# Chunked attention and feed-forward block: mean by a running sum, variance by squares on ScalarE, key/query turns two head pairs at once, first mem values as fp32

## The chip, the cores and the metric

One core of one Trainium2 chip. The metric is the device time of one execution in microseconds (us), the median of several runs. The span of a profile, from its first to its last instruction, is about 1.7 us shorter than the same run's time (246.6 against 248.29). Compare spans with spans and medians with medians.

A ratio in this document is the mean time of one kernel's fast runs over that of the kernel before in the same rounds, so it is not quite the ratio of the two medians quoted beside it.

## The reference

Attention over chunks of 32 rows. Each chunk sees 8 memory keys, 16 rows to the left, its own 32 and 8 to the right. Then comes a layer norm without bias and a feed-forward of 512 to 2048 to 512, with a residual. Sizes: 4 batches, 8 heads, 768 rows, 64 per head.

```python
k_full = np.concatenate([mem_k, k_ctx], axis=2); v_full = np.concatenate([mem_v, v_ctx], axis=2)
a = softmax(scale * q_c @ k_full^T); out_c = a @ v_full          # per chunk of 32 rows (condensed)
mu = mean(x); var = mean((x - mu)**2)
xn = (x - mu) / np.sqrt(var + 1e-06) * g_ln
out = x + np.maximum(xn @ w_ch1, 0.0) @ w_ch2
```

## The kernel before

The 24 tiles of 128 rows are worked in eight units of three. While a unit's feed-forward runs on TensorE (16 "up" steps, one for each 128 of the 2048 hidden columns, then 12 "down" steps), the attention of the next unit's tiles is woven in at fixed steps. Instructions stand in program order on each engine, so one that waits holds back those behind it. The parts that the change touches:

```python
def kq_block(b, j, g0, g1, kind):            # one pair of heads
    if kind == "att":
        p = slot("att")                      # one PSUM tile of two banks
        pk, pq = as16(p[:, 0, :]), as16(p[:, 1, :])
    else:
        pk, pq = as16(slot("mm")[:, :]), as16(slot("mm")[:, :])
    turn_kq(pk, k16[b % 2], j, 96)           # TensorE: transposes of keys
    turn_kq(pq, q16[b % 2], j, 96)           # ... of queries
    keep_k(...)                              # VectorE: copies to KT
    for par in range(2):
        keep_q(nc.scalar.copy, ...)          # ScalarE: copies to QZ

def values(b, t, xi):
    # ... 16 value products into an att slot, 65 columns a head, the 65th the sum of weights
    nc.vector.reciprocal(out=r, in_=...)
    nc.vector.tensor_tensor(out=x, in0=p, in1=r, op=ALU.mult)
    nc.vector.bn_stats(out=bst[i], in_=x)
    nc.vector.bn_aggr(out=m, in_=bst[i])
    nc.vector.scalar_tensor_tensor(out=xn[i], in0=x, scalar=m[:, 0:1], in1=g_row,
                                   op0=ALU.subtract, op1=ALU.mult)
    # root(), later on GpSimd: rstd = (m[:, 1] + 1e-6) ** -0.5, used in the last down step
```

A "turn" is a transpose on TensorE. PSUM is the memory that TensorE writes its products to. Its "slots" go round: two of two banks (att) for scores, values and turns, four of one bank (mm) for the feed-forward. In the lines below, KT and QZ are the turned keys and queries, AT the exps of the scores, V the values, xs and xn a tile's attention before and after the norm, xT the turned xn, rT the relus, w1c and w2c the feed-forward's weights (w1 and w2), and busy the zeros of the filler products. The prologue loads keys, queries, memory values and V, puts the memory values into V with a DMA from SBUF to SBUF (V<-memv), runs three tiles of attention, and fills TensorE's idle time with products of zeros (`stay_busy`).

The softmax here doesn't subtract the row's maximum and nothing guards it: scores larger than these inputs give would overflow.

Of the kernel before, what the change touches and what calls it, by code (L numbers as in the profile page):

```python
# [15 lines left out]
def kernel(  # L16
# [12 lines left out]
    nc = tc.nc  # L29
# [15 lines left out]
    memk16 = sb.tile([128, 2, 64], FP16, name="memk16")  # L45
    memv16 = sb.tile([72, B, H, HD], FP16, name="memv16")[64:72, :, :, :]
    memKT = sb.tile([128, B * 4, 8], FP16, name="memKT")
    g_row = sb.tile([128, 512], FP32, name="g_row")
# [17 lines left out]
    osb = [sb.tile([128, 512], FP32, name=f"osb{i}") for i in range(3)]  # L66
    bst = [sb.tile([128, 6], FP32, name=f"bst{i}") for i in range(3)]
    mv = [sb.tile([128, 2], FP32, name=f"mv{i}") for i in range(6)]
    veps = [sb.tile([128, 1], FP32, name=f"veps{i}") for i in range(3)]
    rstd = [sb.tile([128, 1], FP32, name=f"rstd{i}") for i in range(9)]  # L70
    rec = [sb.tile([128, 2, 4], FP32, name=f"rec{i}") for i in range(2)]

# [17 lines left out]
    def as16(t):  # L90
        return t.bitcast(FP16)
# [110 lines left out]

    def kq_block(b, j, g0, g1, kind):
        if kind == "att":
            p = slot("att")
            pk, pq = as16(p[:, 0, :]), as16(p[:, 1, :])
        else:
            pk, pq = as16(slot("mm")[:, :]), as16(slot("mm")[:, :])
        turn_kq(pk, k16[b % 2], j, 96)
        turn_kq(pq, q16[b % 2], j, 96)  # L210
        keep_k(pk, b, j, 96, g0 + 1 if g0 else 0, g1)
        for par in range(2):
            keep_q(nc.scalar.copy, pq, b, j, par, 96, g0, g1)

# [19 lines left out]
    def values(b, t, xi):  # L234
        x = xs[xi]
        p = slot("att")
        for h in range(H):
            for gg in range(2):
                c0 = HD * (h % 4)
                nc.tensor.matmul(  # L240
                    out=p[64 * gg : 64 * gg + 64, h // 4, c0 : c0 + HD],
                    lhsT=AT[t % 3][0:KR, gg, h, :],
                    rhs=V[b % 2][0:KR, 2 * t + gg, h, :],
                    start=(h % 4 == 0), stop=(h % 4 == 3), tile_position=(0, 64 * gg),
                )
        r = rec[t % 2]
        nc.vector.reciprocal(out=r, in_=free(p, 64, [[512, 2], [HD, 4]]))  # L247
        nc.vector.tensor_tensor(  # L248
            out=x.rearrange("p (a h d) -> p a h d", a=2, h=4),
            in0=free(p, 0, [[512, 2], [HD, 4], [1, 64]]),  # L250
            in1=free(r, 0, [[4, 2], [1, 4], [0, 64]]),
            op=ALU.mult,
        )
        i, m = t % 3, mv[t]
        nc.vector.bn_stats(out=bst[i], in_=x)  # L255
        nc.vector.bn_aggr(out=m, in_=bst[i])  # L256
        nc.vector.scalar_tensor_tensor(  # L257
            out=xn[i], in0=x, scalar=m[:, 0:1], in1=g_row, op0=ALU.subtract, op1=ALU.mult,
        )

    def root(t, xi):
        i = t % 3
        nc.gpsimd.tensor_scalar(  # L263
            out=veps[i], in0=mv[t][:, 1:2], scalar1=1e-6, scalar2=1.0,
            op0=ALU.add, op1=ALU.mult,
        )
        nc.gpsimd.tensor_tensor(out=rstd[xi], in0=veps[i], in1=mhalf, op=ALU.pow)
# [13 lines left out]

    def stay_busy(n):

        p = slot("mm")
        for _ in range(n):
            nc.tensor.matmul(out=p, lhsT=busy[:, 0:128], rhs=busy, start=True, stop=True)  # L286
# [68 lines left out]
    nc.vector.memset(memv16[:, :, :, 64:65], 1.0)  # L355
    nc.sync.dma_start(out=memk32, in_=dram(mem_k, 0, [[64, 128], [128 * 64, 2], [1, 64]]))
    for h in (0, 4):
        for which in range(2):
            load_kq(0, which, 0, CUT, h, h + 4)
    keep(counts[:, 0:1], counts[:, 0:1], 24, 0.0)  # L360
    keep(counts[:, 1:2], counts[:, 1:2], -88, 0.0)
    make_identity(nc, identity)
    nc.gpsimd.dma_start(
        out=memv16[:, :, :, 0:64], in_=dram(mem_v, 0, [[64, 8], [512, B * H], [1, 64]])
    )
    nc.scalar.copy(out=memk16, in_=memk32)
    stay_busy(10)
    clear_v(0)
    clear_k(0)
    mem_keys()  # L370
    mem_cols(0)
    for par in range(2):
        clear_q(0, par)
    stay_busy(8)
    v_mem(0)
# [14 lines left out]
    load_w1(512, 1024)  # L390
    load_w1(1024, 2048)
    load_kq(0, 0, CUT, 96)
    load_kq(0, 1, CUT, 96)
# [7 lines left out]
    load_w2(3)  # L401

    first_k = [as16(slot("mm")[:, :]) for j in range(4)]
    pair = [slot("att"), slot("att")]
    first_q = [as16(pair[j // 2][:, j % 2, :]) for j in range(4)]
    vec, act = nc.vector.tensor_copy, nc.scalar.copy
    for half in ((0, 1), (2, 3)):
        for j in half:
            turn_kq(first_k[j], k16[0], j, CUT)
        for j in half:  # L410
            turn_kq(first_q[j], q16[0], j, CUT)
        for j in half:
            keep_k(first_k[j], 0, j, CUT, 0, 7, act if j == 2 else vec)
        for j in half:
            for par in range(2):
                keep_q(vec if par and j > 1 else act, first_q[j], 0, j, par, CUT, 0, 6)
        stay_busy(9 if half[0] == 0 else 3)
    nc.vector.memset(mhalf, -0.5)
    scores(0, 0)
    scores(0, 1)  # L420
    stay_busy(3)
    values(0, 0, 0)
    scores(0, 2)
    stay_busy(2)
    values(0, 1, 1)
    stay_busy(3)
    values(0, 2, 2)
    stay_busy(2)
    turn_x(0, 0, 0, "mm")
    stay_busy(6)  # L430
    turn_x(0, 1, 1, "mm")
    stay_busy(6)
    turn_x(0, 2, 2, "mm")
# [5 lines left out]
    for u, tiles in enumerate(units):  # L439
# [7 lines left out]
        def attend(steps):  # L447

            for i, (s0, s1, s2) in enumerate(steps):
                t = following[i]  # L450
                at(s0, scores, t // 6, t % 6)
                at(s1, values, t // 6, t % 6, t % 9)
                at(s2, turn_x, u + 1, i, t % 6)
                at(s2, root, t % 6, t % 9)

        if u == 0:
# [3 lines left out]
            at(11, clear_k, 1)  # L460
            for j in range(4):
                at(11 + 3 * (j // 2), kq_block, 0, j, 6, NG, "att")
# [7 lines left out]
        elif u == 1:  # L470
            for j in range(4):
                at(3 + 5 * (j // 2), kq_block, 1, j, 0, NG, "att")
            for g in range(6, NG):
                at(0, load_v_group, 1, g)
            for which in range(2):
                at(1, load_kq, 2, which)
            attend(((12, 16, 20), (16, 18, 23), (20, 22, 26)))
        elif following:
            steps = [(1 + 7 * i, 5 + 7 * i, 11 + 7 * i) for i in range(3)]
            attend(steps)  # L480
            if u in (2, 4):
                b = u // 2 + 1
                for j, step in enumerate((steps[1][1], steps[2][1], steps[2][1], 23)):
                    at(step, kq_block, b, j, 0, NG, "mm" if j == 1 else "att")
                for h in range(H):
# [48 lines left out]
```

## Time and profile before

| | before |
|---|---|
| median time | 248.62 us (248.06 to 249.05) |
| span of the profile | 246.6 us |
| first value product | 21.29 us |
| first feed-forward product | 31.26 us |
| VectorE, one tile's norm (reciprocal to end of xn) | 2.66 us |
| ScalarE busy | 41% |

The row to start from is TensorE's 93%: nothing off TensorE counts unless TensorE waits for it. The waits are in two places, before 31.26 us and in short stalls after it. The prediction below shows the lines. The share of busy time by engine doesn't tell where they are; the chain in order of time and the list of waits do.

### The profile page before, as it was taken

To read this page: it belongs to the slowest core of one execution; us is meant where nothing else is said; L and a number is where in the kernel's file an instruction comes from. 1 tells how busy PE (TensorE), PEld (TensorE's weight loads), DVE (VectorE), ACT (ScalarE), POOL (GpSimd) and SP (SyncE) were. 2 spreads that over 40 slices of the span, in tenths; PEclk is the share of its full clock that TensorE was granted. 3 is DMA by queue.
4 is the path that set the end of the run, shared out by engine and by line. 5 is a ranking of instruction groups with operands and counts; after the bars stand their busy time and mean duration, and the time that the engine had idled before them with its cause. 6 is when DMAs were issued, how large, how long until landed. Compare 5 with 4: busy or idle time off the path is not lost.

```text
span 246.6 us, 5414 instructions
## 1 busy us (share of the span) xinstructions
PE 228.9 (93%) x2264; PEld 137.9 (56%) x2264; DVE 141.4 (57%) x287; ACT 100.7 (41%) x178; POOL 74.9 (30%) x122
## 2 busy tenths in 40 slices
PE   7765999998989999989999999989999999999992
PEld 2443467655765566655665566655765576547540
DVE  3733868278665757747375637776574457444221
ACT  2353235731585334284554045356453045303300
POOL 7862138627501283303022525220022202220000
PEclk9996799999999999999999999999999999999999
DMA  5999999999995199928930194541100110021012
GB/s 85 138 138 222 209 194 163 194 175 98 179 173 88 45 97 71 48 57 115 214 64 3 48 124 55 33 95 56 43 3 12 73 45 0 4 85 43 0 43 85
DMA packets 44279, 22.29 MB, mean 90 GB/s; under 512 B 32432, under 2 KB 39984, under 8 KB 44208
## 3 DMA queue, kind: packets, MB, share of 16 engines
q0 software_dynamic: 39872, 14.39, 72.1%
q1 hardware_dynamic: 4384, 7.57, 10.7%
q8 instruction: 17, 0.28, 0.5%
q14 instruction: 6, 0.05, 0.1%
HBM read 29.10 MB, written 6.29 MB: 144 GB/s over the span
## 4 chain that ended last, share of the span: by engine, by line
PE 73%; DVE 9%; DMA 7%; ACT 6%; issue 2%; POOL 1%; ACTq 0%; DVEq 0%; POOLq 0%; SPq 0%
PE mm L295 29%; PE mm L312 29%; PE att L173 4%; PE att L240 4%; DMA V<-memv 3%; ACT QZ L198 3%; DMA memv<-in_mem_v_dram 3%; PE att L221 3%; PE mm L286 2%; DVE KT L188 2%; PE att L272 2%; DVE xn L257 2%; DVE bst L255 1%; DVE xs L248 1%; ACT AT L228 1%
## 5 line engine op out<-in xcount | busy, mean ns | idle before, releaser
L295 PE MATMUL mm<-xT,w1c 128*128 128x384 f16 x512 | 90.6, 327 | 3.0 <-ACT xT L277 1.9
L312 PE MATMUL mm<-w2c,rT 128*128 128x512 f16 x384 | 89.4, 380 | 0.0
L295 PEld LDWEIGHTS <-w1c 128*128 128x128 f16 x512 | 56.3, 114 | 27.7 <-issue 4.9
L312 PEld LDWEIGHTS <-rT 128*128 128x128 f16 x384 | 35.6, 98 | 37.8 <-ACT rT L301 1.0
L263 POOL TENSOR_SCALAR veps<-mv 128x1 f32<-128x1 f32 x24 | 16.3, 677 | 121.8 <-DVE mv L256 121.6
L303 DVE TENSOR_SCALAR rT<-mm 128x384 f16<-128x384 f32 x64 | 34.9, 555 | 30.1 <-PE mm L295 30.0
L301 ACT ACTIVATE rT<-mm 128x384 f16<-128x384 f32 x64 | 30.9, 489 | 46.2 <-PE mm L295 38.5
L319 DVE SCALAR_TENSOR_TENSOR osb<-mm,rstd,xs 128x512 f32<-128x512 f32 x24 | 17.9, 748 | 40.0 <-issue 20.7
L228 ACT ACTIVATE AT<-att,band 96x512 f16<-96x512 f32 x48 | 30.1, 678 | 11.0 <-PE att L221 10.9
L198 ACT COPY QZ<-att 64x768 f16<-64x768 f16 (+1 forms) x34 | 22.5, 661 | 28.0 <-DVE KT L188 20.8
L277 ACT COPY xT<-att 128x512 f16<-128x512 f16 x21 | 12.3, 584 | 36.2 <-PE att L272 36.1
L109 POOL DMA_DIRECT2D V<-in_v_dram x24 | 18.3, 769 | 12.3 <-DMA w1c<-in_moe_w_ch_dram 7.9
L286 PE MATMUL mm<-busy 128*128 128x512 f16 x52 | 17.0, 471 | 2.6 <-DVE KT L188 1.4
L257 DVE SCALAR_TENSOR_TENSOR xn<-xs,mv,g_row 128x512 f16<-128x512 f32 x24 | 18.0, 752 | 0.9
L221 PE MATMUL att<-QZ,KT 128*128 128x128 f16 x192 | 15.6, 223 | 2.7 <-ACT QZ L198 1.5
L255 DVE BATCH_NORM_STATS2 bst<-xs 128x6 f32<-128x512 f32 x24 | 16.7, 695 | 0.8
L248 DVE TENSOR_TENSOR xs<-att,rec 128x512 f32<-128x512 f32 x24 | 16.6, 692 | 0.8
L188 DVE COPY KT<-att 128x80 f16<-128x80 f16 (+3 forms) x38 | 16.1, 481 | 1.6 <-PE att L173 1.6
L240 PEld LDWEIGHTS <-AT 96*64 96x64 f16 x384 | 8.7, 116 | 14.6 <-issue 8.0
L221 PEld LDWEIGHTS <-KT 128*128 128x128 f16 x192 | 12.8, 100 | 5.8 <-issue 3.1
L240 PE MATMUL att<-V,AT 96*64 96x65 f16 x384 | 11.5, 204 | 5.0 <-DMA V<-memv 3.6
L247 DVE RECIPROCAL rec<-att 128x8 f32<-128x8 f32 x24 | 4.9, 203 | 17.9 <-PE att L240 17.0
(52 smaller groups left out, 126.9 us busy)
## 6 DMA issues: line engine op xcount, KB each, us to landing
out_dram<-osb SPq DMA_DIRECT2D x24, 256.0 KB, 2.0
V<-in_v_dram POOLq DMA_DIRECT2D x36, 96.0 KB, 7.4
k<-in_k_dram POOLq DMA_DIRECT2D x3, 768.0 KB, 10.5
q<-in_q_dram POOLq DMA_DIRECT2D x3, 768.0 KB, 14.2
w2c<-in_moe_w_ch_dram POOLq DMA_DIRECT2D x4, 512.0 KB, 17.7
w1c<-in_moe_w_ch_dram POOLq DMA_DIRECT2D x2, 512.0 KB, 10.2
w1c<-in_moe_w_ch_dram POOLq DMA_DIRECT2D x1, 1024.0 KB, 16.2
k<-in_k_dram POOLq DMA_DIRECT2D x3, 256.0 KB, 5.7
```

The source lines that it names most:

```text
L188: copy(out=free(KT[b % 2], j * KC + 24 + 32 * ga + 8 * lo, [[KR, gb - ga], [8, m], [1, 8]]), in_=free(pv, lo, [[8, gb - ga], [1, m], [n, 8]]),
L198: copy(out=free(QZ[b % 2][rows, j, g0, par, :], 0, [[128, g1 - g0], [8, 8], [1, 8]]), in_=free(pv[rows, :], 8 * g0, [[8, g1 - g0], [1, 8], ...
L221: nc.tensor.matmul(out=p[:, gg, 128 * j : 128 * j + 128], lhsT=KT[b % 2][:, j, KR * g : KR * g + 128], rhs=QZ[b % 2][:, j, g, :, :], start ...
L228: nc.scalar.activation(out=free(a, 32 * c, [[512, 2], [64, 8], [1, 32]], KR), in_=free(p, 32 * c, [[512, 2], [64, 8], [1, 32]], KR), func= ...
L240: nc.tensor.matmul(out=p[64 * gg : 64 * gg + 64, h // 4, c0 : c0 + HD], lhsT=AT[t % 3][0:KR, gg, h, :], rhs=V[b % 2][0:KR, 2 * t + gg, h, ...
L255: nc.vector.bn_stats(out=bst[i], in_=x)
L257: nc.vector.scalar_tensor_tensor(out=xn[i], in0=x, scalar=m[:, 0:1], in1=g_row, op0=ALU.subtract, op1=ALU.mult,)
L286: nc.tensor.matmul(out=p, lhsT=busy[:, 0:128], rhs=busy, start=True, stop=True)
L295: nc.tensor.matmul(out=p, lhsT=free(w, i, [[4, 128]]), rhs=xT[u % 2][:, dt, 0 : 128 * n], start=(dt == 0), stop=(dt == 3),)
L301: nc.scalar.activation(out=o, in_=p, func=ACTF.Relu)
L303: nc.vector.tensor_scalar(out=o, in0=p, scalar1=0.0, scalar2=None, op0=ALU.max)
L312: nc.tensor.matmul(out=p, lhsT=rT[hc][:, 128 * i : 128 * i + 128], rhs=w2c[hc // 4][:, hc % 4, :], start=(hc == 0), stop=(hc == 15),)
```

## The change

The intent is a shorter start and less work on VectorE in the steady part. (1) mem_v of batch 0 comes as fp32 on the hardware queue and is cast by ScalarE; the other batches follow later on the software queue. (2) The norm's mean is the accumulated sum of the product that makes x, and its variance is a Square on ScalarE with an accumulator; bn_stats and bn_aggr go. (3) A key/query block turns two pairs of heads, keys in one PSUM tile, queries in another, at other steps. (4) The prologue's clears, turns, copies and filler products are put in another order and partly cut.

```diff
+    nc.sync.dma_start(out=memv32, in_=dram(mem_v, 0, [[64, 8], [512, H], [1, 64]]))
...
+    nc.scalar.copy(out=memv16[:, 0, :, 0:64], in_=memv32.rearrange("p (h d) -> p h d", h=H))
     stay_busy(10)
+    for par in range(2):
+        clear_q(0, par)
+    clear_k(0)
     clear_v(0)
-    clear_k(0)
...
-        nc.vector.bn_stats(out=bst[i], in_=x)
-        nc.vector.bn_aggr(out=m, in_=bst[i])
         nc.vector.scalar_tensor_tensor(
+            out=x.rearrange("p (h d) -> p h d", h=H),
+            in0=free(p, 0, [[128, H], [1, 64]]), scalar=1.0,
+            in1=free(r, 0, [[1, H], [0, 64]]),
+            op0=ALU.mult, op1=ALU.mult, accum_out=total[i],
+        )
+        nc.vector.tensor_scalar(
+            out=nmean[i], in0=total[i], scalar1=-1.0 / 512, scalar2=None, op0=ALU.mult,
+        )
...
     def root(t, xi):
+        nc.scalar.activation(
+            out=junk, in_=xs[xi], func=ACTF.Square, bias=nmean[i], accum_out=squares[i],
+        )
...
     def kq_block(b, j, g0, g1, kind):
+        pk, pq = slot("att"), None
         if kind == "att":
+            pq = slot("att")
+            pq = [pq[:, i, :] for i in range(2)]
         else:
+            pq = [slot("mm")[:, :] for i in range(2)]
+        for i in range(2):
+            turn_kq(as16(pk[:, i, :]), k16[b % 2], j + i, 96)
+        for i in range(2):
+            turn_kq(as16(pq[i]), q16[b % 2], j + i, 96)
...
     turn_x(0, 0, 0, "mm")
-    stay_busy(6)
+    stay_busy(4)
     turn_x(0, 1, 1, "mm")
...
-                for j, step in enumerate((steps[1][1], steps[2][1], steps[2][1], 23)):
-                    at(step, kq_block, b, j, 0, NG, "mm" if j == 1 else "att")
+                for j, step in ((0, 19), (2, 22)):
+                    at(step, kq_block, b, j, 0, NG, "mm")
```

More of the change, by code (lines that the diff above doesn't have):

```diff
@@ L46 @@
     memv16 = sb.tile([72, B, H, HD], FP16, name="memv16")[64:72, :, :, :]
+    memv32 = sb.tile([72, 512], FP32, name="memv32")[64:72, :]
     memKT = sb.tile([128, B * 4, 8], FP16, name="memKT")
@@ L66 @@
     osb = [sb.tile([128, 512], FP32, name=f"osb{i}") for i in range(3)]
-    bst = [sb.tile([128, 6], FP32, name=f"bst{i}") for i in range(3)]
-    mv = [sb.tile([128, 2], FP32, name=f"mv{i}") for i in range(6)]
+    total = [sb.tile([128, 1], FP32, name=f"total{i}") for i in range(3)]
+    nmean = [sb.tile([128, 1], FP32, name=f"nmean{i}") for i in range(3)]
+    squares = [sb.tile([128, 1], FP32, name=f"squares{i}") for i in range(3)]
+    junk = sb.tile([128, 512], FP16, name="junk")
     veps = [sb.tile([128, 1], FP32, name=f"veps{i}") for i in range(3)]
     rstd = [sb.tile([128, 1], FP32, name=f"rstd{i}") for i in range(9)]
-    rec = [sb.tile([128, 2, 4], FP32, name=f"rec{i}") for i in range(2)]
+    rec = [sb.tile([128, 8], FP32, name=f"rec{i}") for i in range(2)]
     att = [ps.tile([128, 2, 512], FP32, name=f"att{i}") for i in range(2)]
@@ L203, in kq_block @@
     def kq_block(b, j, g0, g1, kind):
+        pk, pq = slot("att"), None
         if kind == "att":
-            p = slot("att")
-            pk, pq = as16(p[:, 0, :]), as16(p[:, 1, :])
-        else:
-            pk, pq = as16(slot("mm")[:, :]), as16(slot("mm")[:, :])
-        turn_kq(pk, k16[b % 2], j, 96)
-        turn_kq(pq, q16[b % 2], j, 96)
-        keep_k(pk, b, j, 96, g0 + 1 if g0 else 0, g1)
-        for par in range(2):
-            keep_q(nc.scalar.copy, pq, b, j, par, 96, g0, g1)
+            pq = slot("att")
+            pq = [pq[:, i, :] for i in range(2)]
+        else:
+            pq = [slot("mm")[:, :] for i in range(2)]
[3 more added lines that the diff above has]
+            turn_kq(as16(pq[i]), q16[b % 2], j + i, 96)
+        for i in range(2):
+            keep_k(as16(pk[:, i, :]), b, j + i, 96, g0 + 1 if g0 else 0, g1)
+        for i in range(2):
+            for par in range(2):
+                keep_q(nc.scalar.copy, as16(pq[i]), b, j + i, par, 96, g0, g1)
     def scores(b, t):
@@ L238, in values @@
             for gg in range(2):
-                c0 = HD * (h % 4)
+                c0 = 128 * (h % 4)
                 nc.tensor.matmul(
@@ L245, in values @@
                 )
-        r = rec[t % 2]
-        nc.vector.reciprocal(out=r, in_=free(p, 64, [[512, 2], [HD, 4]]))
-        nc.vector.tensor_tensor(
-            out=x.rearrange("p (a h d) -> p a h d", a=2, h=4),
-            in0=free(p, 0, [[512, 2], [HD, 4], [1, 64]]),
-            in1=free(r, 0, [[4, 2], [1, 4], [0, 64]]),
-            op=ALU.mult,
-        )
-        i, m = t % 3, mv[t]
-        nc.vector.bn_stats(out=bst[i], in_=x)
-        nc.vector.bn_aggr(out=m, in_=bst[i])
+        r, i = rec[t % 2], t % 3
+        nc.vector.reciprocal(out=r, in_=free(p, 64, [[128, H]]))
+        nc.vector.scalar_tensor_tensor(
+            out=x.rearrange("p (h d) -> p h d", h=H),
+            in0=free(p, 0, [[128, H], [1, 64]]), scalar=1.0,
+            in1=free(r, 0, [[1, H], [0, 64]]),
+            op0=ALU.mult, op1=ALU.mult, accum_out=total[i],
+        )
+        nc.vector.tensor_scalar(
+            out=nmean[i], in0=total[i], scalar1=-1.0 / 512, scalar2=None, op0=ALU.mult,
+        )
         nc.vector.scalar_tensor_tensor(
-            out=xn[i], in0=x, scalar=m[:, 0:1], in1=g_row, op0=ALU.subtract, op1=ALU.mult,
+            out=xn[i], in0=x, scalar=nmean[i], in1=g_row, op0=ALU.add, op1=ALU.mult,
         )
@@ L262, in root @@
         i = t % 3
+        nc.scalar.activation(
+            out=junk, in_=xs[xi], func=ACTF.Square, bias=nmean[i], accum_out=squares[i],
+        )
         nc.gpsimd.tensor_scalar(
-            out=veps[i], in0=mv[t][:, 1:2], scalar1=1e-6, scalar2=1.0,
-            op0=ALU.add, op1=ALU.mult,
+            out=veps[i], in0=squares[i], scalar1=1.0 / 512, scalar2=1e-6,
+            op0=ALU.mult, op1=ALU.add,
         )
@@ L280, in turn_x, with stay_busy @@
         )
-    def stay_busy(n):
-        p = slot("mm")
+    def stay_busy(n, p=None):
+        p = slot("mm") if p is None else p
         for _ in range(n):
@@ L362 @@
     make_identity(nc, identity)
-    nc.gpsimd.dma_start(
-        out=memv16[:, :, :, 0:64], in_=dram(mem_v, 0, [[64, 8], [512, B * H], [1, 64]])
-    )
     nc.scalar.copy(out=memk16, in_=memk32)
+    nc.scalar.copy(out=memv16[:, 0, :, 0:64], in_=memv32.rearrange("p (h d) -> p h d", h=H))
     stay_busy(10)
+    for par in range(2):
+        clear_q(0, par)
+    clear_k(0)
     clear_v(0)
-    clear_k(0)
     mem_keys()
     mem_cols(0)
-    for par in range(2):
-        clear_q(0, par)
-    stay_busy(8)
+    stay_busy(5)
     v_mem(0)
@@ L391 @@
     load_w1(1024, 2048)
+    nc.gpsimd.dma_start(
+        out=memv16[:, 1:B, :, 0:64],
+        in_=dram(mem_v, H * 512, [[64, 8], [512, (B - 1) * H], [1, 64]]),
+    )
     load_kq(0, 0, CUT, 96)
@@ L401 @@
     load_w2(3)
+    vec, act = nc.vector.tensor_copy, nc.scalar.copy
     first_k = [as16(slot("mm")[:, :]) for j in range(4)]
-    pair = [slot("att"), slot("att")]
-    first_q = [as16(pair[j // 2][:, j % 2, :]) for j in range(4)]
-    vec, act = nc.vector.tensor_copy, nc.scalar.copy
-    for half in ((0, 1), (2, 3)):
-        for j in half:
-            turn_kq(first_k[j], k16[0], j, CUT)
-        for j in half:
-            turn_kq(first_q[j], q16[0], j, CUT)
-        for j in half:
-            keep_k(first_k[j], 0, j, CUT, 0, 7, act if j == 2 else vec)
-        for j in half:
-            for par in range(2):
-                keep_q(vec if par and j > 1 else act, first_q[j], 0, j, par, CUT, 0, 6)
-        stay_busy(9 if half[0] == 0 else 3)
+    first = slot("att")
+    first_q = [as16(first[:, 0, :]), as16(first[:, 1, :])]
+    for j in range(2):
+        turn_kq(first_k[j], k16[0], j, CUT)
+    for j in range(2):
+        turn_kq(first_q[j], q16[0], j, CUT)
+    for j in range(2):
+        keep_k(first_k[j], 0, j, CUT, 0, 7)
+        for par in range(2):
+            keep_q(act, first_q[j], 0, j, par, CUT, 0, 6)
+    spare = att[(turn["att"] + 1) % 2][:, 0, :]
+    stay_busy(3, spare)
+    first_q += first_k[0:2]
+    for j in range(2, 4):
+        turn_kq(first_k[j], k16[0], j, CUT)
+    for j in range(2, 4):
+        turn_kq(first_q[j], q16[0], j, CUT)
+    for j in range(2, 4):
+        keep_k(first_k[j], 0, j, CUT, 0, 7, act if j == 2 else vec)
+    for j in range(2, 4):
+        for par in range(2):
+            keep_q(act if j == 2 else vec, first_q[j], 0, j, par, CUT, 0, 6)
     nc.vector.memset(mhalf, -0.5)
+    stay_busy(3, spare)
     scores(0, 0)
     scores(0, 1)
-    stay_busy(3)
+    stay_busy(4)
     values(0, 0, 0)
     scores(0, 2)
+    stay_busy(1)
+    values(0, 1, 1)
     stay_busy(2)
-    values(0, 1, 1)
+    values(0, 2, 2)
     stay_busy(3)
-    values(0, 2, 2)
-    stay_busy(2)
     turn_x(0, 0, 0, "mm")
-    stay_busy(6)
+    stay_busy(4)
     turn_x(0, 1, 1, "mm")
-    stay_busy(6)
+    stay_busy(4)
     turn_x(0, 2, 2, "mm")
@@ L453, in attend @@
                 at(s2, turn_x, u + 1, i, t % 6)
-                at(s2, root, t % 6, t % 9)
+                at(min(s2 + 1, 27), root, t % 6, t % 9)
         if u == 0:
@@ L460 @@
             at(11, clear_k, 1)
-            for j in range(4):
+            for j in (0, 2):
                 at(11 + 3 * (j // 2), kq_block, 0, j, 6, NG, "att")
@@ L470 @@
         elif u == 1:
-            for j in range(4):
-                at(3 + 5 * (j // 2), kq_block, 1, j, 0, NG, "att")
+            for j in (0, 2):
+                at(2 + 2 * j, kq_block, 1, j, 0, NG, "att")
             for g in range(6, NG):
@@ L476 @@
                 at(1, load_kq, 2, which)
-            attend(((12, 16, 20), (16, 18, 23), (20, 22, 26)))
+            attend(((11, 16, 20), (15, 18, 23), (19, 22, 26)))
         elif following:
             steps = [(1 + 7 * i, 5 + 7 * i, 11 + 7 * i) for i in range(3)]
+            if u in (2, 4):
+                steps[2] = (15, 19, 22)
             attend(steps)
```

## The prediction

> **What bounds the kernel now.** First the page: busy time by engine.
>
> ```profile
> PE 228.9 (93%) x2264; PEld 137.9 (56%) x2264; DVE 141.4 (57%) x287; ACT 100.7 (41%) x178; POOL 74.9 (30%) x122
> ```
>
> TensorE is near full and the change leaves its products alone, apart from fewer filler products in the prologue. So only the stretches where TensorE does nothing useful can be won. There are two kinds: the prologue, and short stalls later. The chain that ended last, in order of time, shows the prologue:
>
> ```profile
> 4.61 0.24 POOL identity masks.py:199
> 4.85 7.62 DMA memv<-in_mem_v_dram
> 12.55 8.61 DMA V<-memv
> 21.29 0.65 PE att L240 x16
> ...
> 30.62 0.59 ACT xT L277
> 31.26 7.96 PE mm L295 x48
> ```
>
> Two DMAs in a row, mem_v into its fp16 tile and from there into V, take 16.2 us. The first value product waits for them until 21.29. The feed-forward's first product starts at 31.26. Everything TensorE does before that is small or filler. The 10 us between are VectorE's, by the timeline of the first tile:
>
> ```profile
> 22.06 0.21 DVE L247 RECIPROCAL rec<-att 128x8 f32<-128x8 f32 x1 [5.78 <-PE att L240]
> 22.30 0.69 DVE L248 TENSOR_TENSOR xs<-att,rec 128x512 f32<-128x512 f32 x1
> ...
> 23.03 0.69 DVE L255 BATCH_NORM_STATS2 bst<-xs 128x6 f32<-128x512 f32 x1
> ...
> 23.75 0.18 DVE L256 BATCH_NORM_AGGREGATE mv<-bst 128x2 f32<-128x6 f32 x1
> ...
> 23.97 0.75 DVE L257 SCALAR_TENSOR_TENSOR xn<-xs,mv,g_row 128x512 f16<-128x512 f32 x1
> ```
>
> That is 2.66 us a tile (22.06 to 24.72), three tiles to 29.87, then a turn and a copy. Third, who waited for whom, over the whole span:
>
> ```profile
> ACT QZ L198 <- DVE KT L188: 20.8, 10, 4.4
> ...
> PE att L240 <- DMA V<-memv: 3.6, 1, 3.6
> ```
>
> and TensorE's own waits from 60 us on:
>
> ```profile
> PE att L240 <- ACT AT L228: 1.4, 2, 0.7
> PE mm L295 <- ACT xT L277: 1.3, 3, 0.7
> PE att L221 <- ACT QZ L198: 1.1, 1, 1.1
> PE mm L295 <- DVE rT L303: 0.5, 1, 0.5
> ```
>
> These idle times understate the loss, as the modelled ends of matmuls cover part of it. I therefore took, in the trace, the distance from one matmul's start to the next beyond the usual one of its line (0.162 us for the first product, 0.216 for the second). After 31.3 us the excesses above 0.15 us add up to 7.5 us: 1.4 in the first unit (0.54 before a score product, 0.83 at its end), 1.5 in the second (scores wait for the query copies at 72 us), 1.5 and 1.3 in the third and fifth (query copies, then exp, then values, and the xT copy at the end), and 1.8 in five waits for VectorE's relu, behind the norm chain. 7.5 us is all that the steady part can give.
>
> **What the Trainium skill says.** "PSUM — Partial Sum Buffer", section "PSUM bank collisions raise a hardware error": two engines may not be on one bank and quadrant at a time, and software must keep them apart. The trace agrees with the cost: ScalarE's query copies wait 20.8 us for VectorE's key copies, which sit in the other bank of the same tile, so the guard here is by whole tile. "ScalarE: Activation LUTs", section "What ACT_TABLE_LOAD costs": an activation with a per-partition bias takes about 280 ns plus 0.833 ns an element, 0.71 us for 512; the exp of that kind measures 0.678 us here. The page puts a switch of table set at 2.66 us; the trace has one load, 1.28 us, at the start. Its table-set section names relu, copy, identity and abs as members of every set and does not list Square. "VectorE: DVE Perf Modes", section "Two Vector instructions with no wait between them": an operation that writes out its accumulator counts as two instructions; nothing in this trace shows one. "DMA: Bandwidth & Descriptors", section "SWDGE vs HWDGE vs iDMA": the DMA engines go round between the two kinds of queue. The trace agrees only in part: between 13 and 17.8 us the hardware queue, with two issued transfers (V<-memv, and g_row from 13.5), moved no packet while the software queue moved 2512, most below 512 B; from 17.8 us both ran, 228 packets against 452.
>
> **The change, part by part.**
>
> *mem_v of batch 0 as fp32.* It removes the 7.62 us DMA from the path. In its place come an early hardware-queue load, like memk's (issued 0.79, landed 2.8, so about 3.5), and a ScalarE copy of 8x512 elements, about 0.6 us by the copies of 512 (0.584): ready near 4.2 us. V<-memv then waits for the clearing of V, now behind the clearing of QZ (2 x 1.34 and 2 x 0.36 of issue) and of KT: from the rows of these memsets that ends near 7.1 us in place of 4.6. So V<-memv is issued near 7.2 instead of 12.55. If it gets its packets in before V's small loads fill the queue (about 9 us), it lands by 11 to 15 us; if it starves until they are through, about 17 us, it lands near 19.
>
> *Start of keys and queries.* Query pair 2 goes to ScalarE and pair 3 to VectorE, in separate tiles, where four copies alternated from 13.99 to 16.15 us. The second half's turns no longer stand behind nine fillers (10.71 to 12.75) but behind the last query load (landed 11.34). I put the last query copy at 13.3 us against 16.15 and the first exp pair's end at about 15.0 against 18.0.
>
> *Norm.* Per tile it removes 0.69 + 0.18 us from VectorE, adds a tiny scaling (about 0.13, between the 0.06 of a one-column memset and the 0.18 of the aggregate), turns a 0.69 tensor_tensor into a scalar_tensor_tensor (0.75) and adds an accumulator read (about 0.08, guessed). 2.66 becomes about 2.05 us: 0.6 a tile, 14.6 over 24, three of them, 1.8 us, on the prologue's path. ScalarE gets a Square of about 0.75 us a tile, 18 us in all, from 41% to 48% busy; it feeds only rstd, needed some 16 steps later, so it lies beside.
>
> *Prologue's sum.* Early landing: values at 15.1, VectorE's three tiles from 15.9 to about 22, first product near 23, 8.3 us sooner. But w1's last part landed at 29.65 and the DMA queues are full until 80 us; I expect it near 28.8. Its first use is eight steps of 0.65 us after the start, 28.2, and the key/query tails (landed 32.5) are used right after step 11. So some is given back: 7.3. Late landing: values near 19, first product near 26.9, gain 4.4. Between the two I take 6.0.
>
> *Head pairs two at once.* Same turns and copies, but keys lie in one tile and queries in another, so both engines copy at once. In batches 2 and 3 the block moves from steps 12, 19, 19 and 23 to 19 and 22, behind the exps and values that waited (0.86 twice); the last xT copy moves from step 25 to 22 (0.51 and 0.42 at the end); in unit 1 the second block moves from step 8 to 6 (1.5). About 4.3 us of the 7.5 is theirs; I count 3.5, as two blocks in three steps may wait for their PSUM (K copies 2 x 1.14 behind 2.05 of norm, against 4.3 us of TensorE work between: 0.4 twice).
>
> *Relu behind the norm.* The five waits (0.29 three times, 0.30 and 0.65, 1.8 us) lose up to 0.6 each; ScalarE's added work may put some of it back on the other relus, so I count 1.0.
>
> Sum: 6.0 + 3.5 + 1.0 = 10.5. 248.6 - 10.5 = 238.1, say 238.
>
> **Rivals.** (1) V<-memv starves behind V's loads: 3 us of the prologue stay, 240 to 241. For it: no hardware packet in 13 to 17.8 us. Against: it is issued 5.3 us sooner, while large packets run, and with the key/query loads of batch 2 hardware packets did move. (2) DMA is the new bound: w1, w2 and the tails come no sooner, so everything that TensorE saves must stay below their landings. For: the queues' nines up to 80 us. Against: later transfers keep slack: w2's last part landed 47.1 and is first used near 57, batch 1's queries 55.5 against 62.8, so six or seven us fit, with one us to spare at the queries. If they don't, 241. (3) Square needs another table: two loads a tile, 24 x 2 x 1.28 = 61 us more on ScalarE, enough to stall exps and relus; 255 or more. Square is simple, and I give this 2%. (4) ScalarE becomes late for odd relus where exp, copy and Square meet: four PSUM slots give some 2 us of room; cost under 1 us.
>
> **Range and chances.** Early landing with all stalls gone: 248.6 - 7.3 - 6 = 235; late with half of them: 248.6 - 4.4 - 2.5 = 241.7. I widen both ends: 233.5 to 243. Two per cent is 243.6, which takes rivals 1 and 2 together, or 3. Faster 0.87, same 0.11, slower 0.02.
>
> **What would show it.** Right: the first value product near 15 us (or 19), the first feed-forward product at 23 to 27; three tiles of norm at some 2.05 us each; no ACT QZ <- DVE KT wait in the list; no idle TensorE at 107 and 161 us of the old count; Square at about 0.75 us and still one table load. Wrong: V<-memv issued early but landing past 20; a wait of the first product for w1c, or of the turns for k and q; a scalar_tensor_tensor with accumulator over 1 us; more table loads; new waits on the PSUM of the doubled blocks.

## The result, and the profile after

The changed kernel took 237.8 us (median of 4 runs, 237.32 to 239.8) against 248.75 us (248.06 to 249.05; four runs, three of which the table above has). The ratio is 0.9579, with a 95% interval from 0.9519 to 0.9639. The prediction said 238.0 and 233.5 to 243. A second set of runs, later, gave 237.83 us and 0.9568.

By engine, in the page of the changed kernel, TensorE rose to 95% and ScalarE from 41% to 51%; VectorE fell from 141.4 to 124.3 us:

```profile
PE 222.7 (95%) x2251; PEld 136.6 (58%) x2251; DVE 124.3 (53%) x287; ACT 119.5 (51%) x227; POOL 63.6 (27%) x122
```

The timeline of the changed kernel around its first tile; the bracket at the end is the idle time before the row and what ended it:

```profile
6.64 0.86 SPq L131 DMA_DIRECT2D V<-memv  x1
6.83 3.06 POOL L112 DMA_DIRECT2D V<-in_v_dram  x4 [1.89 <-DVE memKT L162]
...
15.02 0.42 PE L249 MATMUL att<-V,AT 96*64 96x65 f16 x15 [0.78 <-DMA V<-in_v_dram]
...
15.56 0.21 DVE L256 RECIPROCAL rec<-att 128x8 f32<-128x8 f32 x1 [3.60 <-PE att L249]
...
15.81 0.69 DVE L257 SCALAR_TENSOR_TENSOR xs<-att,rec 128x512 f32<-128x512 f32 x1
...
16.42 0.08 DVE L257 DVE_READ_ACCUMULATOR xs<-att,rec 128x1 f32 x1
...
16.54 0.15 DVE L263 TENSOR_SCALAR nmean<-total 128x1 f32<-128x1 f32 x1
...
16.73 0.75 DVE L266 SCALAR_TENSOR_TENSOR xn<-xs,nmean,g_row 128x512 f16<-128x512 f32 x1
```

V<-memv is issued 5.9 us sooner (6.64 against 12.55), and no product waits for it any more. What the first value products wait for is now V itself, its small loads from memory. A tile's norm goes from 15.56 to 17.48: 1.92 us against 2.66. The read of the accumulator is an instruction of its own, 0.08 us, but it lies inside the product's own record (15.81 to 16.50). The next instruction starts 0.73 us after the product's start, as it did in the old norm (22.30 to 23.03), so the accumulator cost this chain next to nothing.

TensorE's own waits over the whole changed run (us in total, times, longest; some lines left out):

```profile
PE att L249 <- DMA V<-in_v_dram: 1.7, 3, 0.8
PE mm L307 <- ACT xT L289: 1.3, 2, 0.7
...
PE att L176 <- DVE KT L191: 1.2, 2, 0.6
PE mm L307 <- ACT rT L313: 1.0, 1, 1.0
```

The waits of values for exp and of scores for query copies are gone or small. Two kinds of those shown are new besides V's: a key turn waits for VectorE's key copies (L176), and one first product waits for ScalarE's relu (L313). New and not shown are two waits of turns for query loads, 0.6 and 0.3 us, which the prediction had among its signs of being wrong.

Where the time went is easiest to see by unit. The table gives the length of each unit, from its first feed-forward product to that of the next, from the traces. "Start" is the first feed-forward product of all. The last four columns are experiments that are told below. The eighth unit (25.3 to 25.6 us) is left out. Starts are to be compared with care: a second profile of the changed kernel (experiment 9) had 22.75 in place of 24.02. TensorE's granted clock between 18 and 21 us was 1.00 in it and 0.50 in the first.

| us | before | after | norm alone | norm back | pairs back | one by one |
|---|---|---|---|---|---|---|
| start | 31.26 | 24.02 | 31.19 | 24.79 | 23.52 | 23.64 |
| unit 1 | 28.81 | 28.67 | 28.82 | 28.68 | 29.65 | 29.95 |
| unit 2 | 29.12 | 28.70 | 29.12 | 28.70 | 29.12 | 30.05 |
| unit 3 | 29.04 | 27.89 | 27.63 | 28.92 | 27.63 | 31.48 |
| unit 4 | 24.91 | 24.27 | 24.27 | 24.50 | 24.27 | 24.27 |
| unit 5 | 28.96 | 27.89 | 27.64 | 28.93 | 27.64 | 29.86 |
| units 6 and 7 | 49.13 | 48.56 | 48.56 | 49.06 | 48.56 | 48.56 |

In this profile the start gave 7.2 us and everything after it about 3.8 (215.3 us before, 211.6 after), 11.0 us of span.

### The profile page after: what moved, and what is told of

Read it like the earlier page. It is cut to its first block, busy times and chain, and to the rows that moved or that the text cites. A ratio compares the mean times of both kernels' runs of the same rounds, so it can differ in the third digit from the quotient of the medians.

```text
span 235.6 us, 5407 instructions
## 1 busy us (share of the span) xinstructions
PE 222.7 (95%) x2251; PEld 136.6 (58%) x2251; DVE 124.3 (53%) x287; ACT 119.5 (51%) x227; POOL 63.6 (27%) x122
## 2 busy tenths in 40 slices
DMA packets 44224, 22.30 MB, mean 95 GB/s; under 512 B 32376, under 2 KB 39928, under 8 KB 44152
## 4 chain that ended last, share of the span: by engine, by line
PE 80%; DVE 6%; issue 5%; DMA 3%; ACT 3%; POOL 1%; DVEq 0%
PE mm L307 35%; PE mm L324 30%; PE att L230 4%; PE att L249 4%; DMA V<-in_v_dram 3%; PE att L176 3%; DVE KT L191 2%; ACT QZ L201 2%; PE mm L298 2%; PE att L284 2%; DVE QZ L343 1%; POOL V L112 1%; DVE osb L331 1%; DVE xs L257 1%; PE mm L176 1%
## 5 line engine op out<-in xcount | busy, mean ns | idle before, releaser
L313 ACT ACTIVATE rT<-mm 128x384 f16<-128x384 f32 x64 | 31.1, 490 | 39.5 <-PE mm L307 39.1
L275 POOL TENSOR_SCALAR veps<-squares 128x1 f32<-128x1 f32 x24 | 4.6, 191 | 122.2 <-ACT junk L272 122.0
L191 DVE COPY KT<-att 128x80 f16<-128x80 f16 (+3 forms) x44 | 18.3, 482 | 2.4 <-PE att L176 2.4
L266 DVE SCALAR_TENSOR_TENSOR xn<-xs,nmean,g_row 128x512 f16<-128x512 f32 x24 | 18.0, 752 | 0.9
L272 ACT ACTIVATE junk<-xs,nmean 128x512 f16<-128x512 f32 x24 | 17.4, 726 | 0.1
L257 DVE SCALAR_TENSOR_TENSOR xs<-att,rec 128x512 f32<-128x512 f32 x24 | 16.6, 691 | 0.8
L201 ACT COPY QZ<-att 64x384 f16<-64x384 f16 (+1 forms) x20 | 12.0, 601 | 8.5 <-PE att L176 8.1
L201 ACT COPY QZ<-mm 64x768 f16<-64x768 f16 (+1 forms) x18 | 13.6, 758 | 4.6 <-PE mm L176 4.4
L249 PEld LDWEIGHTS <-AT 96*64 96x64 f16 x384 | 8.7, 112 | 11.4 <-issue 5.9
L230 PE MATMUL att<-QZ,KT 128*128 128x128 f16 x192 | 15.0, 219 | 0.4 <-ACT QZ L201 0.2
L279 POOL TENSOR_TENSOR rstd<-veps,mhalf 128x1 f32<-128x1 f32 x24 | 13.3, 554 | 2.0
```

The lines of the kernel that those rows point to most:

```text
L191: copy(out=free(KT[b % 2], j * KC + 24 + 32 * ga + 8 * lo, [[KR, gb - ga], [8, m], [1, 8]]), in_=free(pv, lo, [[8, gb - ga], [1, m], [n, 8]]),
L201: copy(out=free(QZ[b % 2][rows, j, g0, par, :], 0, [[128, g1 - g0], [8, 8], [1, 8]]), in_=free(pv[rows, :], 8 * g0, [[8, g1 - g0], [1, 8], ...
L230: nc.tensor.matmul(out=p[:, gg, 128 * j : 128 * j + 128], lhsT=KT[b % 2][:, j, KR * g : KR * g + 128], rhs=QZ[b % 2][:, j, g, :, :], start ...
L249: nc.tensor.matmul(out=p[64 * gg : 64 * gg + 64, h // 4, c0 : c0 + HD], lhsT=AT[t % 3][0:KR, gg, h, :], rhs=V[b % 2][0:KR, 2 * t + gg, h, ...
L257: nc.vector.scalar_tensor_tensor(out=x.rearrange("p (h d) -> p h d", h=H), in0=free(p, 0, [[128, H], [1, 64]]), scalar=1.0, in1=free(r, 0, ...
L313: nc.scalar.activation(out=o, in_=p, func=ACTF.Relu)
```

## The experiments

Twelve runs were made, one of them of the changed kernel again. All were correct. Each was timed in rounds with the kernel before on the same chip (247.98, 248.18 and 248.47 us in the three sets).

### 1 and 2. The norm taken back, and the norm alone

```diff
# norm_back: the changed kernel, with
-  scalar_tensor_tensor(..., accum_out=total[i]); tensor_scalar(nmean...); Square in root()
+  tensor_tensor; bn_stats; bn_aggr; root() on mv[t]
# norm_only: the kernel before, with the opposite edit
```

> The changed kernel with the old norm (bn_stats, bn_aggr, tensor_tensor; root on mv), all else changed. Theory: VectorE's chain of a tile goes from 1.92 back to about 2.65 us; the prologue's three chains are on the path from the first tile on, so the first feed-forward product moves from 24.0 to about 26.0, and some 1.5 us of relu waits return in the later units: about 241.3 us. Rival (V's loads set the prologue, VectorE is off the path elsewhere): under 238.8.

Measured: 242.15 us (240.86 to 242.59), ratio 0.9749; 4.3 us over the changed kernel.

> The kernel before with only the new norm (and value columns at stride 128, root a step later). Theory: 2.2 us in the prologue (3 x 0.74) and about 1.5 us of relu waits: about 245.0 us. Rival (beside other work, or ScalarE's Square costs as much as it saves): 247.5 or more.

Measured: 243.75 us (243.24 to 244.43), ratio 0.9816 (0.9795 to 0.9836); about 4.2 us under the kernel before by the medians.

Both rivals fall. But in the kernel before the way is not the expected one. In the run with the norm alone VectorE was through with its third tile at 28.38 us in place of 29.87, and still the first feed-forward product started at 31.19, as before. TensorE's timeline of this run shows why:

```profile
27.09 0.39 PE L277 MATMUL mm<-identity,xn 128*128 128x128 f16 x4
27.31 1.46 PE L291 MATMUL mm<-busy 128*128 128x512 f16 x6
28.61 0.39 PE L277 MATMUL mm<-identity,xn 128*128 128x128 f16 x4
28.83 1.46 PE L291 MATMUL mm<-busy 128*128 128x512 f16 x6
30.13 0.39 PE L277 MATMUL mm<-identity,xn 128*128 128x128 f16 x4
31.19 1.14 PE L300 MATMUL mm<-xT,w1c 128*128 128x384 f16 x6 [0.68 <-ACT xT L282]
```

The turns of x stand behind six filler products each, and there is no idle time between them. The fillers set the start now. So all of this run's gain lies in the later units: in the table, the third and fifth fall from 29.0 to 27.6 us with nothing but the norm changed, by 1.4 and 1.3, the fourth by 0.6, the sixth and seventh by 0.3 each. TensorE's waits from 60 us on in this run, against the four that the prediction shows for the kernel before, say where from:

```profile
PE att L223 <- ACT QZ L200: 1.1, 1, 1.1
PE mm L300 <- ACT xT L282: 0.7, 1, 0.7
PE att L242 <- ACT AT L230: 0.4, 2, 0.2
```

Values waited 1.4 us for exp and now wait 0.4; the waits for xT fall by 0.6, those for VectorE's relu are gone.

In the changed kernel, which has four fillers there in place of six, the norm's share of the prologue does show. With the norm taken back, the third turn of x waits 1.3 us for VectorE, and the first feed-forward product starts at 24.79; in experiment 9, the changed kernel with the same granted clock of 1.00 from 18 to 24 us, it starts at 22.75. That is the 2.0 us that was expected.

### 3 and 4. mem_v taken back, and mem_v alone

```diff
# memv_back: the changed kernel, with
-  early fp32 load of batch 0 + ScalarE copy; batches 1 to 3 later
+  one software-queue load of all four batches, before V's loads
# memv_only: the kernel before, with the opposite edit
```

> The changed kernel with mem_v loaded for all batches by the software queue as before. Theory: V<-memv is issued near 12.5 us again, moves no packet until V's small loads are through, lands near 20 to 21 us; first value product near 21, first feed-forward product near 28.5: about 242.5 us. Rival (V's own loads, landed 15 to 18.7 us, bound the prologue by themselves): at most 1 us over 237.8.

Measured: 242.23 us (242.15 to 242.37), ratio 0.9762; 4.4 us over the changed kernel. In this run's chain of waits up to the first value product the transfer stands again, with its old length:

```profile
12.50 8.61 DMA V<-memv
21.11 0.14 issue
21.24 0.65 PE att L248 x16
```

The first feed-forward product came at 29.2, near the expected 28.5.

> The kernel before with only the fp32 load of batch 0's mem_v and its ScalarE copy. Theory: V<-memv is issued near 4.8 us and lands by about 11; the first value product then waits for exp (18.0 us) in place of 21.3; about 3.2 us less, 245.5 us. Rival (the transfer starves behind the loads whatever its issue): 248 or more.

Measured: 244.86 us (244.8 to 244.88), ratio 0.9867; 3.1 us under the kernel before. The first value product, at 17.99, waited for exp, as expected:

```profile
17.99 0.46 PE L241 MATMUL att<-V,AT 96*64 96x65 f16 x16 [0.32 <-ACT AT L229]
```

So the transfer's wait was real (21.29 less 17.99 is 3.3 us), and the next thing behind it in the old order were scores and exp. In the changed kernel, with the new start of keys and queries, the value products come at 14 to 15 us.

### 5 and 6. Key/query blocks as before, and with only the tiles as before

```diff
# pairs_back: the changed kernel, with kq_block and its steps of the kernel before
-  for j, step in ((0, 19), (2, 22)): at(step, kq_block, b, j, 0, NG, "mm")
+  for j, step in enumerate((12, 19, 19, 23)): at(step, kq_block, b, j, 0, NG, ...)
# one_by_one: the changed kernel at its new steps, but inside a block
+  for j in (j0, j0 + 1): keys and queries of one pair in one att tile, as before
+  (batches 2 and 3: pair 1 in two mm tiles, as before)
```

> The changed kernel with key/query blocks one head pair at a time at the old steps, in the old tiles; mem_v, prologue and norm as changed. As the prediction had it, 3.5 us of stalls come back: 241.3 us. Rival, formed after the run with the norm alone (whose third and fifth units already last 27.6 us against 27.9 of the changed kernel): the regrouping gives about 0.4 us in the second unit and takes 0.25 in the third and fifth each, so within 0.6 us of 237.8.

Measured: 238.09 us (237.0 to 239.57), ratio 0.9601 (0.955 to 0.9651). Against the changed kernel's 0.9568 (experiment 9) that is 0.8 us more, give or take 1.3: nothing clear of noise. The rival holds, and the prediction's 3.5 us for the regrouping falls. The table has the parts: unit 2 is 0.4 us longer without the regrouping, units 3 and 5 are 0.26 and 0.25 shorter. Unit 1 is longer in this run for another reason, a wait of 0.7 us for w1. By the prediction's own measure (the distance from one matmul's start to the next beyond the usual one), the regrouping took away 1.5 us of scores' waits in unit 2 and put 1.1 us for ScalarE's relu there, behind four query copies in a row. In units 3 and 5 it took away 0.37 us each and put 0.76 us for PSUM there.

> The changed kernel at its new steps, but each pair with keys and queries in one tile as before. If it is the separate tiles that count, ScalarE's query copies wait for VectorE's key copies again: the waits return to some 15 us in all and the time rises by 1 us or more. If it is the steps, or neither: within 0.6 us of the changed kernel.

Measured: 246.03 us (245.12 to 246.95), ratio 0.991: 8.2 us worse than the changed kernel, much more than expected. The list of waits of this run has 15.0 us of ScalarE behind VectorE's key copies, as expected:

```profile
ACT QZ L201 <- DVE KT L191: 15.0, 9, 3.6
...
PE att L176 <- ACT xT L284: 2.7, 2, 1.4
```

But with the old tiles at the old steps the same wait stood at 17.4 us (below) and cost nothing. What costs is TensorE's own wait: in units 3 and 5 the key turns of the two blocks come 1.2 and 1.5 us late. By what ended these waits, they find no free att slot, since the tiles before them are held by query copies and by the copy of xT behind these.

```profile
ACT QZ L201 <- DVE KT L191: 17.4, 10, 2.9
```

Units 3 and 5 last 31.5 and 29.9 us against 27.9. In unit 3 the granted clock fell as well, to 0.95 over the unit, which makes up most of its 1.6 us over unit 5. So the new steps need the new tiles, and the pair of them is worth nothing against the old pair.

### 7. Square done twice

```diff
         nc.scalar.activation(out=junk, in_=xs[xi], func=ACTF.Square, bias=nmean[i], accum_out=squares[i])
+        nc.scalar.activation(out=junk, in_=xs[xi], func=ACTF.Square, bias=nmean[i], accum_out=squares[i])
```

> The changed kernel with every Square done twice: 24 x 0.91 = 22 us more on ScalarE. If Square lies beside TensorE's work, within 0.6 us of 237.8. If ScalarE is late for the odd relus where exp, copy and Square meet, 2 us or more over it, with TensorE's first products waiting for ScalarE's relu.

Measured: 239.83 us (238.34 to 240.22), ratio 0.9649; 2.0 us over. ScalarE's busy time rose by 18.9 us (119.5 to 138.3) and not by 22, since the read of an accumulator starts before the record of its Square ends. Both theories hold, in different places. From unit 2 on, the unit lengths are the changed kernel's to 0.03 us (28.7, 27.89, 24.28, 27.9 and so on): there Square lies wholly beside. In unit 1, three tiles' Squares stand on ScalarE together, in front of the first relus, and TensorE loses 2.1 us:

```profile
29.49 0.85 ACT L316 ACTIVATE rT<-mm 128x384 f16<-128x384 f32 x2
30.00 0.48 PE L310 MATMUL mm<-xT,w1c 128*128 128x384 f16 x2 [1.92 <-ACT rT L316]
```

### 8. The norm alone with fewer fillers

```diff
# norm_only, and
-    stay_busy(6)
+    stay_busy(2)        # before the second and the third turn of x
```

> The run with the norm alone, whose VectorE was through 1.5 us sooner in the prologue but whose first feed-forward product came no sooner (31.19), now with 2 filler products instead of 6 between the turns of x. If the fillers held it up: first product near 29.5 and about 1.6 us below that run, 242.1. If not (w1 or the granted clock): within 0.5 us of it.

Measured: 242.23 us (241.85 to 242.89), ratio 0.976 against 0.9816 of the run with the norm alone; 1.5 us. The first product came at 28.77, and the third turn of x no longer stood behind fillers. So the fillers did hold the norm's share of the prologue. How much of the 1.5 us is the norm's is not shown: the granted clock from 24 to 31 us was 0.91 in this profile against 0.78 in the other. And fewer fillers with the old norm were not tried; there VectorE was through at 29.87 and the third turn started at 30.20, so they might give 0.3 us by themselves.

### 9 and 10. The changed kernel again, and with fewer fillers

```diff
# fewer_fill: the changed kernel, and
-    stay_busy(4)
+    stay_busy(1)        # before the second and the third turn of x
```

> The changed kernel once more, for comparison on this chip: 237.5 to 238.5 us, ratio near 0.958.

Measured: 237.83 us (237.16 to 237.96), ratio 0.9568 (0.9551 to 0.9585). In this profile the fillers ran at the full clock (1.00 between 18 and 21 us, against 0.50) and the first feed-forward product started at 22.75 us, 1.27 sooner than in the first profile of the same kernel. The span was 236.1 us, not less than 235.6: unit 1 took 29.8 us instead of 28.7, and unit 2 29.3 instead of 28.7. TensorE's waits between 20 and 60 us of this run:

```profile
PE mm L307 <- DMA w1c<-in_moe_w_ch_dram: 0.9, 1, 0.9
PE att L176 <- DMA q<-in_q_dram: 0.4, 1, 0.4
```

w1's last part landed at 29.03 us, and the ninth up step stood until then. The query turns of unit 2 stood for 0.6 us by the distance of starts.

> The changed kernel with 1 filler in place of 4 between the turns of x. Without anything else in the way the first feed-forward product comes near 22.8 instead of 24.0 and the time falls by 1.2 us. If w1's last part (landed near 29) is now the bound, the ninth up step waits about 1 us for it and the gain is under 0.5 us.

Measured: 238.55 us (237.88 to 239.4), ratio 0.9601: no gain at all. The first product started at 22.96; then TensorE waited for w1 and, in unit 2, for queries (0.65 and 0.95 us beyond the usual distance of starts). In both runs what the start had gained was lost again to loads, so the DMA bounds the prologue now, as the prediction's second rival had it. As a test of the fillers alone this run is not clean: the second load of queries also held the prologue's turns for 1.4 us (0.6 in the first profile of the changed kernel), and the first value product came at 15.70.

### 11 and 12. Three waits taken away, and a try at the DMA bound

```diff
# three: the changed kernel, and
+  batch 1: keep_q of a block's second pair two steps after the block
+  "mm" blocks: turn the queries before the keys
-  attend(((16, 19, 22), (17, 21, 24), (19, 23, 27)))
+  attend(((16, 19, 22), (17, 21, 24), (19, 23, 26)))
# best: three, and
-  stay_busy(4) before the second and third turn of x;  load_w1(1024, 2048); memv 1:B; key/query tails
+  stay_busy(1);  load_w1(1024, 1536); key/query tails; load_w1(1536, 2048); memv 1:B
```

> The changed kernel with three waits taken away: in the second unit the query copies of a block's second pair come two steps later, so odd relus run between (1.4 us of waits); in the third and fifth the query turns come before the key turns (0.76 each); the first unit's last turn of x one step earlier (0.84). Theory (each wait is on the path): 3.0 to 3.7 us under the changed kernel, about 234.3. Rival (they only move to the next wait): under 1.5 us.

Measured: 235.76 us (234.76 to 236.71), ratio 0.9501 (0.9482 to 0.952) against 0.9568: under the changed kernel by 2.1 us in the medians and 1.7 in the ratios, between the theory and the rival. In its profile the waits aimed at are gone. Left are 0.6 us at the ninth up step, for w1 (landed 28.85), and three of 0.3 to 0.5 us in unit 2; units 3 and 5 take 27.23 us instead of 27.89. This kernel has the lowest median of the study.

> The kernel with those three, 1 filler, and w1's last part loaded in two halves with the key/query tails between them, so that each lands before its first use. Theory (both the fillers and w1's landing held the prologue): 1.0 to 1.5 us under the kernel with the three alone, about 233 us, no wait for w1c. Rival (DMA throughput bounds it in any order): within 0.5 us of it.

Measured: 236.53 us (236.06 to 237.91), ratio 0.953 (0.9505 to 0.9555): 0.8 us over the three alone in the medians, with intervals that overlap. The expected gain of 1.0 to 1.5 us did not come. TensorE's timeline:

```profile
21.89 0.32 PE L318 MATMUL mm<-xT,w1c 128*128 128x384 f16 x1 [0.67 <-ACT xT L300]
22.59 5.39 PE L318 MATMUL mm<-xT,w1c 128*128 128x384 f16 x32 [0.37 <-DMA w1c<-in_moe_w_ch_dram]
30.88 0.52 PE L318 MATMUL mm<-xT,w1c 128*128 128x384 f16 x2 [2.90 <-DMA w1c<-in_moe_w_ch_dram]
```

The ninth up step needs only the half that landed at 25.2 us. Its first product ran, and its second waited until 30.88, when the other half, now behind the tails, had landed (30.84). The very first step does the same with the two halves of w1's first tile: one product, then a wait to 22.59, the second half landing at 22.54. Both halves lie in one tile with four row blocks. The pattern fits a guard that takes a load's whole address range, gaps included, so that a product on the second row block waits for both halves. That is read from the two waits; a run with a tile for each half would test it and was not made.

## Why the prediction was right

The total was right almost to the digit (238.0 against 237.8), by a sum whose terms were not.

- **V<-memv and the start: right, a little small.** Of its two cases the early one came: first product "near 23" and a gain of 7.3, measured 24.02 and 7.2 us (22.75 and 8.5 in the second profile). The text took 6.0 between the cases. The transfer's packets ran from 9.0 to 11.4 us, before most of V's small packets. Experiments 3 and 4 show both directions of it.
- **What the values wait for: not named.** The prediction had exp at 15.1 us. Keys and queries were sooner than it said: the last query copy ended at 11.83, not 13.3, and the first pair of exps at about 13.7, not 15.0. The wait was for V's own loads, issued at 6.83 instead of 5.56, since GpSimd waited 1.89 us for VectorE, whose clears now come later. The time came out the same by luck.
- **The DMA as next bound: right.** The prediction gave back 1 us in the early case for w1's landing near 28.8. It landed at 28.96 and 29.03 in two profiles of the changed kernel, and a start 1.27 us sooner gave no shorter span (236.1 against 235.6).
- **The norm chain: right in size, and in place only with the fillers cut.** 2.05 us a tile was predicted and 1.92 measured: the product with accumulator took 0.69, not 0.75, the accumulator read lay inside it, where 0.08 was added, and the scaling took 0.153, not 0.13. "Three of them, 1.8 us, on the prologue's path" does not hold in the kernel before, where fillers held TensorE. In the changed kernel it does: 2.0 us of start (experiment 1). But units 1 and 2 were 1.15 and 0.63 us shorter in the run with the old norm than in experiment 9, where TensorE waits for w1 and for queries, so the loads took most of it back.
- **The regrouping: wrong.** This is the step that failed: "About 4.3 us of the 7.5 is theirs; I count 3.5" (the parts it names add up to 4.15). No gain from it could be measured (experiment 5). The values' wait for exp and the wait for the xT copy in the third and fifth units were put down to the grouping of head pairs. They were the end of a chain that begins on VectorE. In the third unit of the kernel before, a tile's xn ends at 102.88 us, the key copies follow it on VectorE, ScalarE's query copies follow them, then a relu, exp, and the value products. The chain in order of time:

```profile
103.02 1.14 DVE KT L188 x2
...
105.04 0.79 ACT QZ L198
...
106.62 1.26 ACT AT L228 x2
...
107.92 0.45 PE att L240 x16
```

  With the norm alone changed, in the old tiles at the old steps, these waits shrank or went (experiment 2). The prediction saw the last link and took the cure for it to be there. In the second unit the regrouping did take the wait away, but put another of nearly its size there.
- **The relu behind the norm: mis-sized.** 1.0 us was counted for the norm after the start; the norm gave 3.9 (215.3 us to 211.4 with the norm alone). All 1.8 us of relu waits went; the other 2.1 us are the chain told above. The two terms together were 4.5 and measured 3.8, so the errors cancelled.
- **Square: right beside, a little small.** 0.75 us was predicted. A Square took 0.726 and its accumulator read 0.192, but they overlap, and together they hold ScalarE for 0.82 us. ScalarE's busy time came to 119.5 us where the prediction's 18 more give 118.7; the share is 51% and not 48% because the span is shorter. There is still one table load, so rival 3 falls. Rival 4's wait of TensorE for an odd relu came, 1.1 to 1.25 us against under 1, in unit 2. But what stands before the relu there is four query copies in a row, which the regrouping put there, and no Square.
- **Doubled blocks waiting for PSUM: right, 0.76 instead of 0.4 each,** twice.

The shares of the parts do not add up: mem_v alone gives 3.1 us and the norm alone 4.2, of 10.9. What remains, 3.6 us, must come from what else changed, the start of keys and queries and the fewer fillers, or from parts that need each other. Fewer fillers under the new norm gave 1.5 (experiment 8); the start of keys and queries was not run alone, so its share is not shown.

## What to carry to other kernels

When TensorE waits at the end of a chain over several engines, look at the first link, not at the last: the cheapest cure for a wait on ScalarE here was less work on VectorE in front of it. Filler products that cover a wait become the wait once it is shortened, so cut them along with it. And separate a part by running it alone and by taking it back, even when the total came out as predicted.

## What the Trainium skill lacked or had wrong

- "DMA: Bandwidth & Descriptors", section "SWDGE vs HWDGE vs iDMA": it has the DMA engines go round between the two kinds of queue. Here the hardware queue moved nothing while a dense run of small software packets went: between 13 and 17.8 us of the kernel before, 0 hardware packets against 2512, with two hardware transfers issued. V<-memv's first packet came 5.4 us after its issue (12.55 to 17.95). In the changed kernel, with V's loads not yet dense, it came 2.3 us after (6.64 to 8.98), and 225 hardware packets moved against 964 between 8.4 and 11.6 us. The section states no such starvation; what caused it was not tested.
- "ScalarE: Activation LUTs", section "What it computes" names an accumulator output without a cost. The read of it is an instruction of its own, 0.192 us each; the Square itself took 0.726 us for 512 elements. The read starts 0.1 us before the Square's record ends, so a pair holds ScalarE for 0.82 us, 19.6 us for the 24. The section on table sets doesn't list Square; with exp, relu and copy it needed no second table load.

```profile
L272 ACT ACTIVATE junk<-xs,nmean 128x512 f16<-128x512 f32 x24 | 17.4, 726 | 0.1
...
L272 ACT ACTIVATION_READ_ACCUMULATOR junk<-xs,nmean 128x1 f32 x24 | 4.6, 192 | 0.0
```

- "VectorE: DVE Perf Modes", section "Two Vector instructions with no wait between them", is right that an accumulator output is two instructions. The second takes 0.083 us, inside the first's record: the next instruction starts 0.733 us after the first with an accumulator, 0.725 without. No page has the time of a scalar_tensor_tensor: 0.691 us for 512 fp32 elements with PSUM and a broadcast operand and an accumulator, 0.752 with two SBUF operands.
- No page has the time of GpSimd's operations on one column: the same line of the norm, a tensor_scalar on 128x1, took 0.677 us as add then multiply on the aggregate's second column, and 0.191 us as multiply then add on the sum of squares. The cause was not looked for; it was off the path.
